# Attention and maxout FFN on one core: the first batch's K and Q by casting half-sequence loads and 32x32 turns on VectorE, with the work order written anew

## The chip, the cores and the metric

The kernel runs on one core of a Trainium2 chip. The metric is the device time of one launch in microseconds (us), the median of several runs; less is better. Engines are named as in the profile: PE (TensorE matmul), PEld (its weight load), DVE (VectorE), ACT (ScalarE), POOL (GpSimd) and SP (SyncE, which here only issues DMAs).

## The reference

Attention over 4 batches, 8 heads, 768 positions and head width 64. "Retrieval" heads (heads 0, 2 and 6 of this draw; the flags are an input) are causal; the others are causal and keep only the first 4 positions (the sink) and a window of the last 64. The result, laid out as 3072 tokens of 512, goes through an FFN that takes the maximum of three products:

```python
scores = scale * np.matmul(q, k.transpose(0, 1, 3, 2))
scores = np.where(mask[None, :, :, :], scores, -1000000000.0)
a = np.exp(scores - max); a = a / (np.sum(a, axis=-1, keepdims=True) + 1e-09)
x = np.matmul(a, v)                       # then tokens x (heads * 64)
h = np.maximum(np.maximum(x @ w1, x @ w2), x @ w3)
out = h @ w_out
```

Inputs and output are fp32; the kernel computes its products in fp16 with fp32 sums.

## The kernel before

**Tiles.** A batch is cut in two halves of 384 positions. A task t is one half of one batch with four heads: t = 4 * batch + 2 * half + quad, 16 tasks in all. Each has two pairs of heads, i = 0 and 1. The scores of a task are taken in units u (two in a first half, four in a second), each a few 128-row blocks of keys against up to 384 queries.

**Steps of a task.** K and Q must stand with the head width on the partitions. `scores` (matmul at L441) writes PSUM tiles "st" (two buffers, or single banks "st1"); ACT takes the exp into "pt" (L452). The mask is added before the exp for t = 0 and 1, as a matmul with the identity (L425); for the others the exp is multiplied by 0 or 1 afterwards (`masks`, L479), on POOL or, for eight listed cases, on DVE. `prep_v` casts v into "va" and multiplies it by the head's flag into "vf" (L392, L394). `av` multiplies pt with va or vf (L495), DVE takes the reciprocal (L503) and the product "x" (L505). x is transposed to "xT" by a DMA (L514), or by PE with a copy for t = 0, 1 and 3 (`turn_x`, L527, L531). Once a half's four pairs are in xT, a generator `ffn` is queued: 18 units of four matmuls (L338), of which those with w1 are copied by ACT into "acc" (L346) and the other two maxed by DVE (L349), then three outputs of six matmuls (L364), copied out by ACT (L370) and stored. `fill(n)` runs the next n steps of the queued generators. PSUM outside "st" comes from four banks that turn round.

**K and Q.** Batches 1 to 3: `load` casts four heads to fp16 in the DMA (POOL's queue), 768 positions at once, and `turn` transposes 32x32 blocks on DVE (L190), four instructions for a task's K and Q; the head width then stands as 2 x 32 rows, and scores run on four row tiles of 32 rows with two matmuls each (r = 0, 1). Batch 0: `load_pairs` loads fp32 pairs of heads on SP's and ACT's queues (second half on POOL's), `cast_pair` casts them to fp16 on ACT, POOL or DVE (L139), `turn_pair` transposes by PE (L157) and copies from PSUM (L162); scores run on two row tiles of 64 rows.

**Order.** The kernel is scheduled by hand: each engine runs its instructions in the order in which the Python emits them and waits at each for its inputs. The first four score units and the work around them are written out as calls; from t = 2 on a table `PROGRAM` holds for each score unit how many FFN units are due and what else to emit, and a running sum hands out `fill`. SP's loads of later v wait behind a "gate", a tiny DMA that reads a pt tile. POOL also issues the casting DMAs, in order with its other work.

Of the kernel before, what the change touches and what calls it, by code (L numbers as in the profile page):

```python
# [38 lines left out]
APART = [(0, 0, 1, (384,), 128, 0), (1, 1, 1, (384,), 128, 0)] + MASKED[1][1:]  # L39

# [11 lines left out]
def kernel(  # L52
# [31 lines left out]
    G = 4  # L84
# [4 lines left out]
    BY_DMA = (2, 4, 5, 6, 7, 8, 9, 10, 11, 12, 13, 14, 15)  # L89

    consts = ctx.enter_context(tc.tile_pool(name="consts", bufs=1))
    stage = ctx.enter_context(tc.tile_pool(name="stage", bufs=3))
    half16 = ctx.enter_context(tc.tile_pool(name="half16", bufs=3))
# [27 lines left out]
    def load_pairs(half, hp, n, engines, alone=False):  # L121
        for nm, src, eng in zip(("ks", "qs"), (k, q), engines):
            st = stage.tile([P, 4, HB, D], FP32, tag=nm, name=nm)
            m = 2 if alone else 2 * n
            for h in range(0, 2 * n, m):
                eng.dma_start(
                    out=st[:, h : h + m],
                    in_=src[
                        0, 2 * hp + h : 2 * hp + h + m, half * HALF : (half + 1) * HALF
                    ].rearrange("h (p j) d -> p h j d", p=P),  # L130
                )
            for i in range(n):
                staged.setdefault((half, hp + i), []).append(st[:, 2 * i : 2 * i + 2])

    def cast_pair(half, hp, engines):
        cast[half, hp] = []
        for nm, src, op in zip(("kn", "qn"), staged.pop((half, hp)), engines):
            x = half16.tile([P, HB, 2, D], FP16, tag=nm, name=nm)
            op(out=x, in_=src.rearrange("p h j d -> p j h d"))  # L139
            cast[half, hp].append(x)  # L140

    def of_pair(hp):
        return KQs[0, hp // 2].rearrange("p i t two -> p i (t two)")[
            :, hp % 2
        ].rearrange("p (i t) -> p i t", i=2)

    def turn_pair(half, hp, *engines):
        if (0, hp // 2) not in KQs:
            KQs[0, hp // 2] = qkt.tile([P, 2, S, 2], FP16, tag="KQ", name="KQ")
        xs = cast.pop((half, hp))  # L150
        n = 2 // len(engines)
        for part, op in enumerate(engines):
            tr = bank([P, 1024], FP16, "tr")
            for i in range(n):
                for j in range(HB):
                    c = i * HALF + j * P
                    nc.tensor.transpose(  # L157
                        tr[:, c : c + P],
                        xs[part + i][:, j].rearrange("p h d -> p (h d)"),
                        ident,  # L160
                    )
            op(  # L162
                out=of_pair(hp)[
                    :, part : part + n, half * HALF : (half + 1) * HALF
                ].rearrange("p i (t j) -> p i t j", j=HB),
                in_=tr[:, 0 : n * HALF].rearrange("p (i j t) -> p i t j", i=n, j=HB),
            )


# [12 lines left out]
    def turn(b, qd, i, part):  # L182
        if (b, qd) not in KQs:
# [5 lines left out]
        src = st[:, i, j0:j1].rearrange("c j d -> c (j d)").bitcast(FP32)  # L189
        nc.vector.transpose(  # L190
            out=dst.rearrange("c (p j) -> c j p", j=n)[:, j0:j1],
# [11 lines left out]
    def load_v(b, half, engines=None):  # L203
        engines = engines or (nc.sync,) * HB
        vs = stage.tile([P, H, HB, D], FP32, tag="vs", name="vs")
        for j in range(HB):
            r0 = half * HALF + j * P
            engines[j].dma_start(
                out=vs[:, :, j], in_=v[b, :, r0 : r0 + P].rearrange("h p d -> p h d")
            )  # L210
        staged_v[b, half] = vs
# [515 lines left out]
```

The softmax here doesn't subtract the row's maximum and nothing guards it: scores larger than these inputs give would overflow.

## Time and profile before

| | us |
|---|---|
| median of 3 runs | 200.86 (200.83 to 201.8) |
| span of the profiled execution | 199.3 |
| PE / DVE / ACT / POOL busy | 189.7 / 122.5 / 131.7 / 123.3 |
| first exp of scores (ACT L452) | starts 8.59 |
| first FFN's w1 products (PE L338) | start 17.8, run on from 18.66 |
| second FFN's start (PE L338) | 50.08 |
| last PE instruction ends | 195.7 |

The profile has the span of its execution, first to last instruction, but no other time for it; the median lies 1.56 us above. A row of the page such as "PE 7897..." gives the busy share in tenths over 40 slices of 5 us. A row of a timeline is: start, duration, engine, line, operation, output <- input, shapes, count, and in brackets the idle time ahead of it with what ended it. Rows with a count above one merge instructions that run on.

### The profile page before, as it was taken

The numbers are of one execution on the slowest core, as the hardware profiler recorded it, in microseconds if no ns is written. First come the engines' busy times: TensorE is split into PE (matmuls) and PEld (weight loads), VectorE is DVE, ScalarE is ACT, GpSimd is POOL, SyncE is SP. The second block draws the span as 40 slices with busy tenths as digits, with TensorE's granted clock in tenths as the row PEclk, the third lists the DMA queues.
The fourth block names the chain that finished last, engine by engine and source line by source line (L and its number), as shares of the span: only waits on it lengthen the run. The fifth ranks groups of instructions, "written<-read, shape, count | busy, mean of one in ns | idle before, by whom it ended". The sixth has DMA issues, their size and how long they took to land.

```text
span 199.3 us, 5133 instructions
## 1 busy us (share of the span) xinstructions
PE 189.7 (95%) x2059; PEld 109.5 (55%) x2059; DVE 122.5 (61%) x241; ACT 131.7 (66%) x206; POOL 123.3 (62%) x154
## 2 busy tenths in 40 slices
PE   7897999996999999999999999999999999999992
PEld 2455555545566465574555565565555565755652
DVE  2698587999687829861555649961555234543540
ACT  4585798786966776676786775848758769323221
POOL 3599159789887906787969635799847447400000
PEclk9999999999999999999999999999999999999999
DMA  6999999994949991904359995513410250023004
GB/s 182 270 213 245 278 238 212 213 202 112 256 81 154 194 274 43 178 0 146 95 101 132 170 254 141 85 26 98 116 23 20 105 76 20 3 64 135 3 0 158
DMA packets 43245, 26.48 MB, mean 133 GB/s; under 512 B 33558, under 2 KB 38230, under 8 KB 43222
## 3 DMA queue, kind: packets, MB, share of 16 engines
q1 hardware_dynamic: 37206, 15.01, 34.9%
q0 software_dynamic: 4784, 10.23, 26.7%
q10 hardware_dynamic: 1232, 0.92, 1.5%
q8 instruction: 16, 0.26, 0.6%
q14 instruction: 7, 0.06, 0.1%
HBM read 25.17 MB, written 6.29 MB: 158 GB/s over the span
## 4 chain that ended last, share of the span: by engine, by line
PE 78%; DVE 8%; ACT 4%; DMA 3%; issue 3%; POOL 2%; SPq 1%; ACTq 0%; POOLq 0%; DVEq 0%
PE yy L338 43%; PE yy L364 12%; PE st L441 10%; PE oacc L495 8%; DVE KQ L190 4%; PE yst L338 3%; ACT pt L452 3%; DMA ks<-in_k_dram 2%; DVE x L505 2%; DMA out_dram<-ot 1%; PE tr L157 1%; PE yst L364 1%; POOL kn L139 1%; DVE hT L349 1%; POOL qn L139 0%
## 5 line engine op out<-in xcount | busy, mean ns | idle before, releaser
L479 POOL TENSOR_TENSOR pt<-pt,mk 128x512 f16<-128x512 f16 (+1 forms) x76 | 80.6, 1084 | 34.8 <-ACT pt L452 34.7
L452 ACT ACTIVATE pt<-st 128x1024 f16<-128x1024 f32 (+3 forms) x99 | 83.1, 894 | 19.4 <-PE st L441 18.6
L349 DVE TENSOR_TENSOR acc<-yy,acc 128x384 f16<-128x384 f32 x45 | 25.1, 558 | 28.9 <-PE yy L338 19.3
L338 PE MATMUL yy<-xT,w1t 128*128 128x384 f16 x180 | 36.1, 327 | 0.1
L338 PE MATMUL yy<-xT,w0t 128*128 128x384 f16 x180 | 35.6, 326 | 0.4 <-DVE xT L531 0.4
L338 PE MATMUL yy<-xT,w2t 128*128 128x384 f16 x180 | 35.7, 327 | 0.0
L346 ACT CAST acc<-yy 128x384 f16<-128x384 f32 x45 | 21.0, 485 | 17.0 <-PE yy L338 10.5
L364 PE MATMUL yy<-woutt,hT 128*128 128x512 f16 (+1 forms) x138 | 32.0, 375 | 0.0
L441 PE MATMUL st<-KQ 32*128 32x384 f16 (+4 forms) x560 | 28.7, 279 | 1.0 <-DVE KQ L190 0.8
L349 DVE TENSOR_TENSOR hT<-yy,acc 128x384 f16<-128x384 f32 x45 | 25.1, 560 | 6.6 <-PE yy L338 4.0
L495 PEld LDWEIGHTS <-pt 128*128 128x128 f16 x672 | 24.0, 97 | 5.3 <-issue 2.1
L190 DVE STREAM_TRANSPOSE KQ<-kq 128x384 f32<-128x384 f32 x24 | 25.7, 1130 | 0.0
L338 PEld LDWEIGHTS <-w0t 128*128 128x128 f16 x192 | 18.2, 98 | 12.9 <-issue 1.0
L495 PE MATMUL oacc<-va,pt 128*128 128x65 f16 x352 | 24.8, 193 | 0.3 <-ACT va L392 0.3
L338 PEld LDWEIGHTS <-w2t 128*128 128x128 f16 x192 | 17.6, 98 | 13.3 <-issue 2.1
L338 PEld LDWEIGHTS <-w1t 128*128 128x128 f16 x192 | 17.2, 98 | 12.8 <-issue 1.3
L370 ACT COPY ot<-yy 128x512 f32<-128x512 f32 x22 | 12.9, 588 | 15.9 <-PE yy L364 9.6
L364 PEld LDWEIGHTS <-hT 128*128 128x128 f16 x150 | 14.0, 98 | 14.6 <-issue 0.3
L441 PEld LDWEIGHTS <-KQ 32*128 32x128 f16 (+1 forms) x560 | 12.2, 93 | 17.8 <-issue 11.5
L495 PE MATMUL oacc<-vf,pt 128*128 128x65 f16 x320 | 21.2, 193 | 0.8 <-POOL vf L394 0.8
L505 DVE TENSOR_TENSOR x<-oacc,rc 128x384 f16<-128x384 f32 x32 | 17.8, 557 | 1.1
L503 DVE RECIPROCAL rc<-oacc 128x6 f32<-128x6 f32 x32 | 6.1, 192 | 20.0 <-PE oacc L495 19.8
(70 smaller groups left out, 129.9 us busy)
## 6 DMA issues: line engine op xcount, KB each, us to landing
out_dram<-ot SPq DMA_DIRECT2D x23, 256.0 KB, 3.1
vs<-in_v_dram SPq DMA_DIRECT2D x21, 256.0 KB, 6.3
kq<-in_k_dram POOLq DMA_DIRECT2D x6, 384.0 KB, 5.6
kq<-in_q_dram POOLq DMA_DIRECT2D x6, 384.0 KB, 8.0
qs<-in_q_dram ACTq DMA_DIRECT2D x4, 192.0 KB, 4.0
ks<-in_k_dram SPq DMA_DIRECT2D x4, 192.0 KB, 3.6
w0t<-in_moe_w_dram POOLq DMA_DIRECT2D x1, 768.0 KB, 7.4
ks<-in_k_dram POOLq DMA_DIRECT2D x2, 384.0 KB, 7.2
```

What stands on the lines that cost most here:

```text
L190: nc.vector.transpose(out=dst.rearrange("c (p j) -> c j p", j=n)[:, j0:j1], in_=src.rearrange("c (j i) -> c j i", i=R),)
L338: nc.tensor.matmul(yy[:, 0:HALF], w_t[wi][:, ks, ni * P : (ni + 1) * P], xT[b, half][ks].rearrange("p a t -> p (a t)"), start=(ks == 0), s ...
L346: nc.scalar.copy(out=acc[ni], in_=yy[:, 0:HALF])
L349: nc.vector.tensor_tensor(out=dst, in0=yy[:, 0:HALF], in1=acc[ni], op=ALU.max)
L364: nc.tensor.matmul(yo[:, 0:n], hT[ns][:, tb * P : (tb + 1) * P], woutt[:, ns, c : c + n], start=(ns == 0), stop=(ns == NNB - 1),)
L370: op(out=ot[:, c : c + n], in_=yo[:, 0:n])
L441: nc.tensor.matmul(sts[g // m][:, g % m, c0 : c0 + n * P], KQ[rows, 0, ki * P : (ki + 1) * P], KQ[rows, 1, t0 : t0 + n * P], start=(c0 == ...
L452: nc.scalar.activation(out=pts[t, i][:, u, h0 : h0 + m, 0:w], in_=st[:, :, 0:w], func=AF.Exp, scale=sc,)
L479: engine.tensor_tensor(out=x, in0=x, in1=m, op=ALU.mult)
L495: nc.tensor.matmul(o[:, qi, hl, 0 : D + 1], pt[:, u, hl, c : c + P], vv[:, 2 * hp + hl, ki, 0 : D + 1], start=(idx == 0), stop=(idx == len ...
L503: nc.vector.reciprocal(out=rc, in_=o[:, :, :, D])
L505: nc.vector.tensor_tensor(out=x, in0=o[:, :, :, 0:D], in1=rc.unsqueeze(3).to_broadcast([P, HB, 2, D]), op=ALU.mult,)
```

## The change

- Batch 0 loads K and Q like the other batches, cast to fp16 by the DMA on POOL's queue, four heads together, but a half sequence at a time (`load_half`). Its source is h p (j d), since the half sequence cuts the heads apart. `load_pairs`, `cast_pair`, `turn_pair` and the pool "half16" go.
- `turn` turns batch 0 on DVE, one instruction for K or Q of a half. All scores run on four row tiles of 32 rows, also pair by pair.
- What was fixed in the code becomes an argument: the engine of a mask product ("k t i u d"), of an FFN copy-out ("f 1 d" or "f 1 a"), the way of xT ("av ... D" by DMA).
- The whole order is one list of items, `PROGRAM`, ahead of it a short list `FIRST`. The loads of w3 (w_t[2]) and w1 (w_t[0]) come in this order; the two others follow later. The flags' broadcast uses an own row of ones. `EARLY` is 0 and has no effect.

In the list, "s t u [i] [b]" is a score unit (of pair i alone; b: single banks), "f 1 e" one FFN step, "turn b q i half" a turn (i: 0 for K, 1 for Q), "v t i ef" a `prep_v` with the engines of its cast and product, "lh half q" a half load, "load b q" a full one, "em" and "m" the mask tables before and after the exp, "w n" a weight.

```diff
+FIRST = "lh 0 0, ir, lh 0 1, v 0 0"
+PROGRAM = (
+    "read, turn 0 0 0 0, flags, far, em 0, w 2, w 0, idle 8, turn 0 0 1 0, em 1, s 0 0 0",
+    "turn 0 1 1 0, s 0 0 1, s 0 1 0 b, v 0 0 pd, turn 0 1 0 0, em 2, s 0 1 1, v 1 0 pp, lh 1 0",
+    "v 1 1 pp, em 3, v 0 1 ad, idle 2, s 1 0 0, av 0 0, s 1 0 1, s 1 1, m 3, av 0 1, x 0 0 a",
+    "av 1 0, w 1, x 0 1 a, av 1 1, x 1 0 d, turn 0 0 0 1, turn 0 0 1 1, x 1 1 a, m 2, f 1 d",
+    "f 1 a, m 1, f 1 d, s 2 0, f 1 a, lh 1 1, f 1 a, load_vp 0 1, m 0, f 1 d, s 2 1, w 3",
+    "load 1 0, f 1 a, load 1 1, f 1 a, f 1 a, k 2 0 1 p, f 1 a, turn 0 1 1 1, turn 0 1 0 1",
+    "s 2 2, f 1 d, k 2 1 1 p, f 1 a, f 1 d, s 2 3 0, k 2 0 2 p, s 2 3 1, k 2 0 3 p, f 1 d",
+    "k 2 1 2 p, f 1 a, s 3 0, f 1 a, f 1 a, s 3 1 1, v 2 0 pd, f 1 d, gate, av 2 0 D, k 3 1 0 p",
+    "v 2 1 ap, turn 1 0 0 0, s 3 1 0, k 2 1 3 p, load_v 1 0, s 3 2 0, k 3 1 1 d, k 3 0 0 d",
...
+    "f 1 a, v 15 0 ad, f 1 d, f 1 a, k 15 1 3 d, f 1 d, k 15 0 3 p, av 15 0 D, av 15 1 D, f 1 d",
+    "f 1 a, f 1 a, f 1 a, f 1 a, f 1 a, x 15 1 a, f 1 d, f 1 a, f 1 a",
+)
...
+    def load_half(half, qd, which="kq"):
+        if (0, qd) not in staged:
+            staged[0, qd] = stage.tile([P, 2, S // R, D], FP16, tag="kq", name="kq")
+        n = HALF // R
+        for i, src in enumerate((k, q)):
+            if "kq"[i] in which:
+                nc.gpsimd.dma_start(
+                    out=staged[0, qd][:, i, half * n : half * n + n].rearrange(
+                        "p j d -> p (j d)"
+                    ),
+                    in_=src[
+                        0, G * qd : G * qd + G, half * HALF : (half + 1) * HALF
+                    ].rearrange("h (p j) d -> h p (j d)", p=R),
+                )
...
     def turn(b, qd, i, part):
...
+        if b == 0:
+            dst = dst[:, part * HALF : (part + 1) * HALF]
+            dst = dst.rearrange("c (p j) -> c j p", p=R)
+        else:
+            dst = dst.rearrange("c (p j) -> c j p", p=R)[:, j0:j1]
...
-        nc.tensor.matmul(flags, base[0:1, 0:P], RT1, start=True, stop=True)
+        nc.tensor.matmul(flags, ones, RT1, start=True, stop=True)
...
-                nc.scalar.copy(out=acc[ni], in_=yy[:, 0:HALF])
+                copy_out[0](out=acc[ni], in_=yy[:, 0:HALF])
...
-            for r in range(1 if b == 0 else 2):
-                for g in range(2 * i, 2 * i + 2) if b == 0 else range(G):
+            for r in range(2):
+                for g in [g for i in pairs for g in (2 * i, 2 * i + 1)]:
```

## The prediction

> **What bounds the kernel now.** I read the page from its head: busy shares, then the slices, then the stretches of time, then the timeline where the slices show holes.
>
> ```profile
> span 199.3 us, 5133 instructions
> PE 189.7 (95%) x2059; PEld 109.5 (55%) x2059; DVE 122.5 (61%) x241; ACT 131.7 (66%) x206; POOL 123.3 (62%) x154
> ...
> PE   7897999996999999999999999999999999999992
> ...
> DVE  2698587999687829861555649961555234543540
> ...
> DMA  6999999994949991904359995513410250023004
> ```
>
> TensorE (PE) is busy 95%, with holes in the first ten slices only, where the DMA row stands at 9 too. Busy time by stretch (PE, PEld, DVE, ACT, POOL; then clock, DMA share, GB/s):
>
> ```profile
> 18.00:37.00 19.00, 18.41 (x163) 10.13 (x162) 14.74 (x27) 15.55 (x25) 12.67 (x16) 1.00 1.13 235
> 37.00:50.00 13.00, 10.79 (x179) 6.34 (x175) 12.72 (x23) 9.54 (x14) 11.02 (x14) 1.00 0.79 169
> 50.00:90.00 40.00, 40.00 (x490) 23.86 (x479) 29.56 (x54) 29.13 (x44) 28.59 (x35) 1.00 0.78 147
> 90.00:170.00 80.00, 79.90 (x905) 45.55 (x904) 41.09 (x80) 59.30 (x90) 56.74 (x65) 1.00 0.50 100
> ```
>
> From 50 us on PE has no hole: nothing can be won there, only lost. From 37 to 50 us VectorE (DVE) is busy 12.72 of 13 us and PE only 10.79, so DVE is the bound. The timeline shows with what:
>
> ```profile
> 39.23 2.08 DVE L190 STREAM_TRANSPOSE KQ<-kq 128x384 f32<-128x384 f32 x2
> 41.84 2.08 DVE L190 STREAM_TRANSPOSE KQ<-kq 128x384 f32<-128x384 f32 x2
> 44.10 3.01 DVE L190 STREAM_TRANSPOSE KQ<-kq 128x384 f32<-128x384 f32 x3
> 48.34 1.12 DVE L190 STREAM_TRANSPOSE KQ<-kq 128x384 f32<-128x384 f32 x1
> ...
> 50.08 2.12 PE L338 MATMUL yy<-xT,w0t 128*128 128x384 f16 x12
> ...
> 54.28 1.16 POOL L479 TENSOR_TENSOR pt<-pt,mk 128x512 f16<-128x512 f16 x1 [0.94 <-ACT pt L452]
> 54.73 0.99 DVE L479 TENSOR_TENSOR pt<-pt,mk 128x512 f16<-128x512 f16 x1 [0.21 <-ACT pt L452]
> ```
>
> Eight turns of batch 1 take about 1.0 us each back to back. The second FFN starts at 50.08, with scores up to t=5, u=0 done. **I measure the change at that mark.** What PE has left there takes to the end, 149.2 us, in either kernel. The last two lines are a DVE mask product of 0.99 us that starts while POOL runs one; at 27.58, POOL idle, it takes 0.42.
>
> The transfers by form:
>
> ```profile
> 8.00:10.00 2.00, 1.87 (x20) 0.87 (x17) 1.95 (x7) 1.41 (x3) 1.36 (x4) 1.00 1.39 218
> 15.00:16.50 1.50, 1.20 (x33) 1.01 (x29) 1.35 (x5) 1.22 (x4) 1.50 (x3) 1.00 1.04 357
> 24.00:27.00 3.00, 2.92 (x27) 1.40 (x26) 2.46 (x6) 2.41 (x3) 1.20 (x3) 1.00 1.15 241
> 36.00:40.00 4.00, 4.00 (x75) 2.61 (x72) 3.97 (x7) 3.01 (x4) 2.40 (x4) 1.00 1.08 213
> ```
>
> The last number is GB/s written: v in 256-byte pieces 218, fp32 K and Q uncast 357, casting loads (weights, K and Q of batch 1) 213 to 241. A cast halves the bytes at some 60% of the rate.
>
> [...] The new loads read h p (j d), slowest dimension 4; all loads before have 128. No trace of before shows such a load.
> [...]
>
> **The change part by part.**
>
> *PE.* 48 K/Q transposes go: 24 before 12 us, beside waits, and 24 from 20.9 to 31 us (0.80 + 0.44 + 0.34 = 1.6 us). Batch 0's scores take the same time: a unit of four heads is 8 matmuls of 64 rows in about 0.6 us before (24.14), 16 of 32 rows in 0.56 after (as at 55.62).
>
> *DVE.* Removed: 7 copies KQ of 0.95, one of 0.56, two casts of 0.54, two xT copies: 9.0 us. Added: 8 turns (8.0 to 9.0), 15 acc copies and 7 ot copies that "f 1 d" puts on DVE (0.5 and 0.6: 11.7), masks from 10 to 33 (23 x 0.42 if free, about 1.0 if blocked: 10 to 23), 5 instead of 2 va casts, 14 instead of 2 vf products (about 8). DVE goes from 122 to about 155 us. ACT loses about 19 us, POOL 32; neither bounds PE in the long run.
>
> *DMA in the opening.* K and Q of batch 0: 3.15 MB at 357 GB/s = 8.8 us before; 1.57 MB at 213 = 7.4 after. The gain is 1.4 us, and w2 now goes ahead of w0 (0.79 MB at 213 = 3.7 us).
>
> **The walk to the mark.** (1) POOL first issues four casting loads (0.54 to 0.59 each, 2.3 us), and its constants (base, kept, ident) come 2.3 us later, so DVE is free at 5.3 instead of 2.9. The first K lands at about 4.5 (issue at 0.8, plus the shortest landing of a kq load, 4.6, less 0.9 for half the bytes). DVE then needs the flags 0.16, turn 1.0, RT/least/far 0.57, two masks 0.65, turn 1.0: 8.7. With 0.6 of PE the first exp is at 9.3 (8.59 before).
>
> (2) v 0 0 on SP shares the engines with four casts, then w2: alone it would be in at 10.7; I take 13.0. "v 0 1 ad" puts a va copy on ACT ahead of the exps of t=1, and these queue behind it: 13.6, then four exps (1.03, 1.03, 0.63, 0.63) with 0.9 of waits for PSUM to 17.8, av, 1/x, transposes and copy to 20.3. The first FFN can complete its sums at 20.3 (18.66 before). w0 lands at about 18, hidden.
>
> (3) From 19.7 (K and Q of the second half) DVE does two turns 2.1, three mask pairs 2.1 and three acc copies 1.5, to 25.4; PE waits for Q's turn and then for PSUM banks, and reaches unit 7 at about 25.5. w1 (23.3) is hidden. Twelve max (0.5), two turns, a vf product and waits for PE bring DVE to the reciprocal of "av 2 0" at 36.4 (38.54 before). POOL's mask products, queued behind DMA issues that wait on earlier landings, start at about 26, early enough.
>
> (4) From there DVE bounds as before: 8 turns 8.3, four 1/x pairs 3.0, three masks (1.3 to 3.0), xT 0.4: 13 to 14.7, so 49.4 to 51.1, and 0.7 for transposes and copy. **The mark comes at about 50.8: +0.7.** The 1.6 us of PE transposes saved vanish, because PE is not what is late.
>
> (5) After the mark DVE carries 36.6 us of work to the 17th unit of the third FFN, over 38 us of PE (97%; 29.56 of 40 before). Worst are that FFN's first nine units: DVE 12, PE 9, and four PSUM banks hold only some 2.6 us. With masks that meet POOL (nine, up to 0.6 each) I take +1.0, bounds 0 and +3. The tail is unchanged: after the last "av" six FFN groups (three units 1.95, three outputs 3.9 us) cover the last xT transfer, as the 5.2 us at 174.91 do now.
>
> Costed at nothing: the flags' own "ones" row (a memset of some 0.1 us in the wait for POOL's constants), the 8 + 2 idle matmuls instead of 10 (PE waits for loads there), and w1's place behind the half loads, which the masks on DVE hide by 2.2 us; were that cover gone, PE would wait at unit 7 for what is missing. v 1 0 is issued behind its gate at about 34 (36.56 before) and shares with casts as before; if it lands after 47, "v 4 1 ap" on ACT holds the copy of "x 3 1", and the mark slips with it.
>
> Sum: 199.3 + 0.7 + 1.0 = 201.0. The median of the runs is 1.56 above the profiled span; with that, 202.6.
>
> **Rivals.**
> - *The loads don't spread (slower still).* [...] a load is 32 packets on each of four engines at 0.139 us (a 1536-byte packet's mean in the records) = 4.4 us instead of 0.9. The first K lands near 7.9, everything follows by 2.4, and the second half's K and Q land at 24 instead of 19: the mark moves by a further 4. 206.5. For: the shape of the source. [...]
> - *DVE never idles (faster).* Its work from 19.7 to the "av 2 0" reciprocal is 14.6 us. If PE's results are always there first, it arrives at 34.4, the masks fall into POOL's pauses (1.3), and the mark comes at 47.8: −2.3. With no loss after, 198.6. It decides this way when the reciprocal starts before about 35.9. For: ACT and POOL are relieved, and the transposes are gone from DVE's wait. Against: acc copies placed behind turns that wait for landings.
> - *Tie.* The mark at 50.1 and nothing lost after: 200.9.
>
> **How the numbers follow.** Slower by the DVE sum (200.9 to 205) 0.44, most of it above 201.9; the loads don't spread 0.22; tie 0.14; faster 0.20. Half a per cent, 1.0 us, is about what a measurement of this kernel can tell from no change. Faster 0.20, same 0.18, slower 0.62. The likeliest case gives 202.6; its own range is 200.9 to 205. The range for 8 in 10 reaches into both outer cases, 199.0 to 207.5.
>
> **What would show it.** Right: the mark between 50 and 52, DVE over 90% busy from 37 to the mark and over 85% in the 40 us after, PE holes after the mark. The loads: 128 packets on four engines would show as a landing over 6 us for kq in the first 10 us. Wrong: the first exp before 8.5, the reciprocal of "av 2 0" before 35.9, or PE without a hole from 47 us on.

## The result and the profile after

The changed kernel takes 217.77 us (median of 4, 216.43 to 219.07) against 200.91 for the kernel before: ratio 1.082, 95% interval 1.0759 to 1.0881. It is slower by 16.9 us, well outside the forecast range of 199.0 to 207.5. Ratios here leave disturbed runs out, so that for one kernel below (e12) the ratio is lower than its median suggests.

The page of the changed kernel, its head and slices:

```profile
span 215.3 us, 5156 instructions
PE 195.6 (91%) x2091; PEld 110.7 (51%) x2091; DVE 147.4 (68%) x298; ACT 115.5 (54%) x167; POOL 95.0 (44%) x122
...
PE   0659889999799999999389999999999999999993
...
DVE  0293395879979879979437975988496766872640
...
PEclk9985599999999999999859999999999999999999
DMA  5999999997923997184991104701416340114004
```

PE now has two holes that before lacks: the first three slices (0, 6 and 5 where before has 7, 8 and 9) and slice 20, at 102 to 108 us. PEclk, the granted clock, falls to half twice; by its records from 14.2 to 27.9 us, and from 106.4 to 113.2 around the end of the second hole. By stretch (PE, PEld, DVE, ACT, POOL, then clock, DMA share, GB/s):

```profile
12.00:28.00 16.00, 14.23 (x123) 7.46 (x123) 8.37 (x21) 7.35 (x12) 10.80 (x17) 0.57 1.13 155
28.00:45.00 17.00, 16.38 (x166) 8.76 (x163) 12.99 (x29) 11.38 (x16) 9.15 (x11) 1.00 1.19 195
45.00:60.00 15.00, 13.72 (x223) 8.38 (x222) 13.33 (x23) 11.85 (x18) 12.11 (x15) 1.00 0.93 210
60.00:98.00 38.00, 38.00 (x443) 21.99 (x442) 33.25 (x64) 25.36 (x37) 20.04 (x25) 1.00 0.64 122
98.00:114.00 16.00, 11.85 (x108) 5.55 (x106) 8.61 (x15) 5.09 (x10) 8.41 (x12) 0.79 0.86 161
```

Where I feared VectorE, from 60 to 98 us, it is busy 33.25 of 38 us and PE has no hole at all. The loss lies ahead of 60 and at 98 to 114. The two ends of the first loss are in the timeline, the issue of the first load by POOL and what DVE waits for:

```profile
1.32 0.86 POOL L177 DMA_DIRECT2D kq<-in_k_dram  x1 [0.81 <-POOLq L627]
...
10.66 0.84 DVE L210 STREAM_TRANSPOSE KQ<-kq 128x384 f32<-128x384 f32 x1 [3.92 <-DMA kq<-in_k_dram]
...
12.89 0.85 DVE L210 STREAM_TRANSPOSE KQ<-kq 128x384 f32<-128x384 f32 x1 [0.34 <-DMA kq<-in_q_dram]
```

The turn of the first K begins 9.3 us after the load's issue. The first FFN products and the mark of the prediction, the second FFN slice, stand in PE's timeline:

```profile
29.39 2.35 PE L376 MATMUL yy<-xT,w0t 128*128 128x384 f16 x12
...
59.59 0.82 PE L376 MATMUL yy<-xT,w0t 128*128 128x384 f16 x4
```

The second loss stands in the timelines of SP, POOL and PE:

```profile
97.17 4.31 SPq L555 DMA_TRANSPOSE xT<-x  x2
...
99.11 0.59 POOL L189 DMA_DIRECT2D kq<-in_k_dram  x1
99.70 0.54 POOL L189 DMA_DIRECT2D kq<-in_q_dram  x1
...
108.32 0.48 PE L376 MATMUL yy<-xT,w0t 128*128 128x384 f16 x1 [4.15 <-DMA xT<-x]
```

The second of the two DMA transposes is issued at about 100 us, when POOL has just issued the cast loads "load 3 0"; it lands 8.6 us later (median of all transposes 2.3), and PE waits 4.15 us for it.

I measure every kernel at four points (us; "rest" runs from the second FFN slice, the prediction's mark, to the end of the span; a star: PE began the FFN, then stopped for the second half of K):

| kernel | first exp | first FFN products | second FFN slice | rest | span | median |
|---|---|---|---|---|---|---|
| before | 8.6 | 17.8 | 50.1 | 149.2 | 199.3 | 200.9 |
| after | 14.5 | 29.4 | 59.6 | 155.7 | 215.3 | 217.8 |
| e1 idle work first | 14.6 | 29.8 | 60.3 | 154.0 | 214.3 | 215.0 |
| e2 load 3 0 late | 12.7 | 22.9* | 59.7 | 150.9 | 210.6 | 211.7 |
| e3 full loads | 12.8 | 28.8 | 59.1 | 154.9 | 214.0 | 216.9 |
| e4 all three | 12.3 | 28.6 | 58.8 | 149.1 | 207.9 | 209.3 |
| e5 e4, hole filled | 12.6 | 30.8 | 61.0 | 149.1 | 210.1 | 209.4 |
| e6 half loads, hole filled | 14.4 | 24.8* | 59.8 | 149.1 | 208.9 | 209.6 |
| e7 e6, 2nd half by heads | 13.8 | 26.0 | 58.8 | 153.6 | 212.4 | 214.1 |
| e8 e7, 1st quad fp32 | 16.9 | 27.2 | 58.9 | 154.6 | 213.5 | 215.2 |
| e9 both quads fp32 | 10.8 | 29.0 | 59.2 | 149.0 | 208.2 | 209.7 |
| e10 e6, 2nd half early | 13.8 | 25.9 | 57.5 | 149.0 | 206.5 | 209.0 |
| e11 e9 by order of need | 13.0 | 28.3 | 58.5 | 149.6 | 208.1 | 209.9 |
| e12 e10, w0 ahead | 13.8 | 32.3 | 62.8 | 148.9 | 211.7 | 209.8 |
| e13 before, no idle work | 8.5 | 17.6 | 49.5 | 149.2 | 198.7 | 201.5 |
| e14 mixed | 10.8 | 33.1 | 63.3 | 149.4 | 212.7 | 214.0 |
| e15 e14, little idle work | 14.2 | 33.3 | 63.5 | 149.2 | 212.7 | 214.6 |
| e16 e14, V ahead | 11.7 | 22.9* | 59.7 | 152.2 | 211.9 | 213.1 |
| e17 before, w0 ahead | 7.6 | 22.0 | 53.6 | 149.2 | 202.8 | 205.3 |

Two columns read like constants. Where no DMA transpose holds PE for more than 0.6 us, the rest is 148.9 to 149.6 in both orders. And in the changed order the second slice follows the first products by 30.2 to 30.5 in ten of the thirteen rows without a star. In e7, e8 and e10 it takes 31.6 to 32.9; in e7 and e10 the clock is half for 3.4 us at the FFN's start, and for e8 the reason was not looked for. So the loss of 16.0 us in the span is the first exp +5.9, from there to the first products +5.7, from there to the slice −2.1, and the rest +6.5.

### The profile page after: what moved, and what is told of

Read it like the earlier page. It is cut to its first block, busy times and chain, and to the rows that moved or that the text cites. A ratio compares the mean times of both kernels' runs of the same rounds, so it can differ in the third digit from the quotient of the medians.

```text
span 215.3 us, 5156 instructions
## 1 busy us (share of the span) xinstructions
PE 195.6 (91%) x2091; PEld 110.7 (51%) x2091; DVE 147.4 (68%) x298; ACT 115.5 (54%) x167; POOL 95.0 (44%) x122
## 3 DMA queue, kind: packets, MB, share of 16 engines
q0 software_dynamic: 8560, 10.24, 30.2%
q1 hardware_dynamic: 36118, 14.23, 28.3%
## 4 chain that ended last, share of the span: by engine, by line
PE 80%; DMA 10%; POOL 3%; ACT 3%; DVE 2%; issue 1%; POOLq 0%; ACTq 0%
PE yy L376 43%; PE st L487 13%; PE yy L412 10%; PE oacc L536 9%; DMA kq<-in_q_dram 5%; DMA xT<-x 4%; PE yst L376 3%; ACT pt L498 2%; PE st L475 2%; POOL pt L520 1%; DMA out_dram<-ot 1%; DVE KQ L210 1%; DVE x L546 1%; POOL vf L444 1%; PE yst L412 1%
## 5 line engine op out<-in xcount | busy, mean ns | idle before, releaser
L520 POOL TENSOR_TENSOR pt<-pt,mk 128x512 f16<-128x512 f16 (+1 forms) x53 | 57.8, 1109 | 46.7 <-ACT pt L498 35.2
L376 PE MATMUL yy<-xT,w0t 128*128 128x384 f16 x180 | 36.7, 332 | 4.2 <-DMA xT<-x 4.2
L396 DVE TENSOR_TENSOR acc<-yy,acc 128x384 f16<-128x384 f32 x45 | 24.9, 559 | 18.4 <-PE yy L376 15.1
L376 PE MATMUL yy<-xT,w2t 128*128 128x384 f16 x180 | 36.4, 331 | 0.0
L210 DVE STREAM_TRANSPOSE KQ<-kq 128x384 f32<-128x384 f32 x32 | 32.7, 1056 | 4.3 <-DMA kq<-in_k_dram 3.9
L487 PE MATMUL st<-KQ 32*128 32x384 f16 (+2 forms) x640 | 32.9, 289 | 1.5 <-DVE KQ L210 1.5
L412 PE MATMUL yy<-woutt,hT 128*128 128x512 f16 (+1 forms) x138 | 31.6, 375 | 0.0
L536 PEld LDWEIGHTS <-pt 128*128 128x128 f16 x672 | 25.2, 99 | 4.4 <-issue 1.4
L536 PE MATMUL oacc<-va,pt 128*128 128x65 f16 x352 | 25.8, 197 | 0.0
L487 PEld LDWEIGHTS <-KQ 32*128 32x128 f16 x640 | 14.4, 94 | 21.6 <-issue 15.5
L393 ACT CAST acc<-yy 128x384 f16<-128x384 f32 x30 | 14.3, 485 | 20.4 <-PE yy L376 15.9
L376 PEld LDWEIGHTS <-w2t 128*128 128x128 f16 x192 | 17.4, 98 | 12.2 <-issue 1.3
L412 PEld LDWEIGHTS <-hT 128*128 128x128 f16 x150 | 13.7, 98 | 16.2 <-issue 1.5
L536 PE MATMUL oacc<-vf,pt 128*128 128x65 f16 x320 | 21.6, 194 | 0.3 <-POOL vf L444 0.3
L546 DVE TENSOR_TENSOR x<-oacc,rc 128x384 f16<-128x384 f32 x32 | 17.8, 558 | 1.2
L520 DVE TENSOR_TENSOR pt<-pt,mk 128x512 f16<-128x512 f16 (+1 forms) x33 | 16.9, 529 | 2.2 <-ACT pt L498 2.2
L444 POOL TENSOR_TENSOR vf<-va,far 128x384 f16<-128x384 f16 x9 | 7.7, 856 | 24.1 <-DVE va L442 12.6
## 6 DMA issues: line engine op xcount, KB each, us to landing
kq<-in_k_dram POOLq DMA_DIRECT2D x4, 192.0 KB, 11.9
w0t<-in_moe_w_dram POOLq DMA_DIRECT2D x1, 768.0 KB, 10.4
```

The source lines that it names most:

```text
L210: nc.vector.transpose(out=dst, in_=src.rearrange("c (j i) -> c j i", i=R),)
L376: nc.tensor.matmul(yy[:, 0:HALF], w_t[wi][:, ks, ni * P : (ni + 1) * P], xT[b, half][ks].rearrange("p a t -> p (a t)"), start=(ks == 0), s ...
L393: copy_out[0](out=acc[ni], in_=yy[:, 0:HALF])
L396: nc.vector.tensor_tensor(out=dst, in0=yy[:, 0:HALF], in1=acc[ni], op=ALU.max)
L412: nc.tensor.matmul(yo[:, 0:n], hT[ns][:, tb * P : (tb + 1) * P], woutt[:, ns, c : c + n], start=(ns == 0), stop=(ns == NNB - 1),)
L444: vf_engine.tensor_tensor(out=vf[j][:, hs, k0:k1, 0:D], in0=vs[:, hs, 0:1] if half == 0 else va[j][:, hs, k0:k1, 0:D], in1=far[:, hs, k0:k ...
```

## The experiments

**The rest of the run, and the first guesses at the start (e1 to e4).** e1 gives PE work from the start; e2 moves one load; e3 replaces the half loads; e4 has all three.

```diff
e1
-    "read, turn 0 0 0 0, flags, far, em 0, w 2, w 0, idle 8, turn 0 0 1 0, em 1, s 0 0 0",
+    "idle 12, read, turn 0 0 0 0, flags, far, em 0, w 2, w 0, idle 12, turn 0 0 1 0, em 1, s 0 0 0",
e2
-    "load 3 0, f 1 d, s 8 1, turn 2 1 1 1,
+    "f 1 d, s 8 1, turn 2 1 1 1,
...
-    "f 1 a, f 1 d, k 8 0 0 d, s 9 1,
+    "f 1 a, f 1 d, load 3 0, k 8 0 0 d, s 9 1,
e3 (and both halves turned at once, ahead of the scores)
-FIRST = "lh 0 0, ir, lh 0 1, v 0 0"
+FIRST = "load 0 0, ir, load 0 1, v 0 0"
```

> Only the idle matmuls are changed: 12 are put ahead of everything on TensorE and the later 8 become 12, so that TensorE has work from the start to about 12 us instead of standing idle until 6.8. In the changed kernel's profile the granted clock is half between 14.8 and 28.5 us. Theory 'the idle start costs the clock, and the clock costs time': the clock stays at 1.0 through that stretch, and the second FFN slice (59.6 us in the changed kernel) starts 3 to 4 us earlier: 213 to 214 us. Rival 'the transfers set the pace of the start': the first FFN products still wait until about 29 us for the loads, the time stays within 1 us of the changed kernel's 217.8 whatever the clock does.

> Only the cast load of the last batch's first quad of heads (load 3 0) is moved, from just before 'av 7 1' with its DMA transpose to some ten items later, so that the transpose (xT of av 7 1, 8.6 us from issue to landing in the changed kernel against a median of 2.3) no longer runs beside a cast load. Theory 'the transpose is held up by the cast load': the transpose lands in 2 to 3 us, TensorE's wait of 4.15 us at 104 to 108 us goes and the half clock at 107 to 114 us behind it: 209.5 to 212 us. Rival 'TensorE has no ready work there anyway, or the late load delays its turns': the wait only moves to another place and the time stays above 216 us.

> The first batch's K and Q are loaded like the other batches' (head outermost merged with the 32 rows to 128, the whole sequence in one transfer for a quad of heads) and turned in both halves at the start; the half-sequence loads are gone. Theory 'four heads outermost put a load on four DMA engines only, and that is most of the loss': K of the first quad, twice as many bytes, lands under 6.5 us after its issue instead of 9.3, the first exponential is at 11 to 13 us instead of 14.5, the first FFN products before 27 us instead of 29.4, and the time is 211 to 215 us. Rival 'it is the bytes and the shared queue, not the spread': the first K lands at over 10 us and the time is 217 us or more.

> The three edits together: whole-sequence loads of the first batch, the idle matmuls from the start, load 3 0 moved later. Theory that the loss is the spread of the loads, the half clock and the wait at 104 us, and that they add: 203 to 207 us. Rival 'they all hide one another behind the same late weights': above 209 us, with the first FFN products no earlier than 27 us.

e1: 215.04 us. The clock was full from 6.9 to 13.7 us, then half all the same until 30.7; the start did not move (slice at 60.3). The rival's account of the start held, but not its time: it said within 1 us of 217.8, and e1 takes 2.8 less. The profiled execution shows 1.7 of that in the rest (3.4 us of half clock behind the late transpose instead of 6.8).

e2: 211.73 us, 6.0 us less than after. The wait at 104 to 108 is gone, and the rest falls from 155.7 to 150.9; of the 1.9 that remain, 1.5 are a smaller wait for xT at 82 us. In e4, e5, e6, e9 and e10 no transpose holds PE, and the rest is 149.0 to 149.1. In e7, e8 and e16 PE waits 2.8, 4.0 and 2.9 us for xT at 83 us. POOL's cast loads of batch 2 and SP's transposes meet ahead of that, but they do so in after, e4 and e6 too, without a wait there; so its cause is open. **That the cast load "load 3 0" makes the DMA transpose beside it late is shown.** By what way it does so is not shown. In after the packets of the first transpose begin 1.2 us after its issue, those of the late one 4.1 us, when 183 of the load's 256 packets have begun.

e2 also runs the start of the changed kernel a second time, since its edit acts only at 100 us. The two executions differ: in e2 the first exp comes at 12.7 (14.5 in after), the clock is full from 11.2 to 28.2 us, where after has half, and from the first exp to the first FFN products it takes 10.3 us instead of 14.9. And yet the second slice comes at 59.7 (59.6 in after). PE had to stop for the second half of K; in the chain of e2 two loads of 192 KB take 21.1 of the first 27.3 us:

```profile
1.32 7.88 DMA kq<-in_k_dram
...
14.07 13.23 DMA kq<-in_k_dram
```

So a full clock alone gained nothing at the slice while the second half landed this late. And single executions of one start differ by nearly 2 us at the first exp, which limits what a single profile below can tell. The turn of the first K begins 7.7 to 9.3 us after the issue in the seven profiles with the same four half loads in front (after, e1, e2, e6, e7, e10, e12); after's is the longest.

e3: 216.93 us, a miss in the total but not in its mechanism. Queue rows of the changed kernel and of e3, in this order:

```profile
q0 software_dynamic: 8560, 10.24, 30.2%
```

```profile
q0 software_dynamic: 4912, 10.23, 25.7%
```

The same bytes take 3648 packets less: in the changed kernel each of the eight half loads adds 384 packets of 4 bytes (3072 of the 3648), and its first data packets run about four at a time (4.0 to 4.4 at 3.9 to 4.9 us, and 16.2 at 8.0 to 8.5, with all four half loads issued). A full load has more: in before the last one of batch 2 shows 16.8 at a time from 67 to 68 us. With full loads the first K, twice the bytes, was there about 5 us after its issue (5.3 in e3, 5.1 in e4, 4.9 in e5), not 7.7 to 9.3; VectorE's timeline of e4, where POOL issues at 1.30:

```profile
6.37 2.09 DVE L206 STREAM_TRANSPOSE KQ<-kq 128x384 f32<-128x384 f32 x2 [0.21 <-DMA kq<-in_k_dram]
```

That one half load keeps to four packets at a time to its end is my estimate from these counts; its later landing is measured. But a full row holds 24 neighbouring positions, so both halves must be turned before the first score: 4.2 us of VectorE instead of 1.7. The first exp came at 12.8, and the FFN hardly earlier: its first products at 28.8 (29.4 in after), where the theory had them before 27.

e4: 209.26 us, above its 203 to 207 and in its rival's range (above 209). The edits do not add: with the rest at 149.1 everything left, 8.7 us, is ahead of the second slice.

**The half clock (e5, e6).** In e3 the page grants the full clock throughout the start:

```profile
PEclk9999999999999999999969999999999999999999
```

Yet the mask matmuls from 11 to 28 us take as long in e3 (first line) as in e4 (second), where PEclk shows 5; in e6 (third) the clock is full:

```profile
L471 PE MATMUL st<-mk,ident 128*128 128x256 f16 x14 | 4.4, 402 | 1.2 <-DVE mk L323 0.6 <-ACT pt L494 0.6
```

```profile
L471 PE MATMUL st<-mk,ident 128*128 128x256 f16 x14 | 4.3, 403 | 1.6 <-DVE mk L323 1.0 <-ACT pt L494 0.6
```

```profile
L475 PE MATMUL st<-mk,ident 128*128 128x256 f16 x16 | 3.1, 274 | 0.8 <-ACT pt L498 0.8
```

402 ns against 274 (275 in before): e3 ran at half clock, and its records merely begin at 29.4 us. The column after the count is the busy sum, then the mean of one. So the clock row is to be checked against a matmul of known size. The stretches at half clock in the records last 3.4 us (e7, e16, e17), 6.8 and 13.7 (after) or 17.1 (e4, e14). What raises the clock again is not shown: in after it stayed at half for 13.7 us, though the profile has PE busy for 100% and 98% of the first two 3.4 us of them, and in e4 it stayed for 17.1 us with one such stretch at 100%; in before the records begin at 7.2 us, at full, behind 3.4 us that were busy 91%. In after and e14 it rose again 1.5 and 1.4 us ahead of the FFN, so it can rise during attention there too.

```diff
e5 (from e4)
-em 0, w 2, w 0, idle 12, turn 0 0 1 0,
+em 0, w 2, w 0, idle 22, turn 0 0 1 0,
e6 (after with load 3 0 late, 12 idle matmuls first)
-em 0, w 2, w 0, idle 8, turn 0 0 1 0,
+em 0, w 2, w 0, idle 27, turn 0 0 1 0,
```

> As the kernel with all three edits, but 22 idle matmuls instead of 12 between the flags and the first scores, so that TensorE has no hole before the first scores at 11.5 us. There the clock fell to half at 12.6 us, after the hole of 9.1 to 11.5, and the matmuls of the first two attention tiles ran at half rate until 29.7 (a mask matmul of 256 columns every 0.21 us). Theory 'the hole lets the clock fall, and the sparse attention matmuls do not raise it again: the start is TensorE at half clock': the clock stays full from 6 us on, the first FFN products start at 21 to 23 us instead of 28.6, the second FFN slice at 51 to 54 instead of 59, and the time is 201 to 204.5 us against 209.3. Rival 'the exponentials and VectorE's turns set the pace there': the first FFN products at 27 us or later, the time above 207.5 us.

> The changed kernel [...] with load 3 0 late, 12 idle matmuls at the start and 27 instead of 8 before the first scores: the clock is kept full there too. Theory 'two limits lie side by side at the start, the half clock and the landing of the second half of K': the clock stays full, but the turn of the second half, which VectorE has ahead of the last copies to xT, still waits for a landing at 27 to 29 us, so the first full FFN stretch starts at 28 to 30 us and the time is 208 to 211 us. Rival 'the half clock alone': first FFN products at 23 to 25 us and a time of 203 to 205.

e5: 209.36 us, no gain. The clock held to 16.5 us. PE then stood twice: 2.86 us, to 18.3, for masks that DVE makes behind its turns of the whole rows, and 2.15 us, to 22.25, for V, which was issued at 1.2 and was there only at 21.6. V is a third gate, which I had not listed.

e6: 209.61 us, as its first theory says. From PE's and DVE's timelines:

```profile
24.83 2.20 PE L376 MATMUL yy<-xT,w0t 128*128 128x384 f16 x12
30.30 0.64 PE L487 MATMUL st<-KQ 32*128 32x384 f16 x16 [3.27 <-DVE KQ L210]
```

```profile
27.89 0.84 DVE L210 STREAM_TRANSPOSE KQ<-kq 128x384 f32<-128x384 f32 x1 [3.19 <-DMA kq<-in_k_dram]
```

At full clock the FFN starts 10.4 us after the first exp (14.9 in after, 16 in e3 and e4), and then PE waits for the second half of K, which POOL issued at 15.9 and which lands at 27.9, 12.0 us later. **Half clock and late second half lie side by side; taking one away leaves the other.**

**The second half of K and Q (e7, e10).** e7 splits each of its loads into four of one head; e10 issues it behind the first half.

```diff
e7
+            for g in range(G if half else 0):
+                nc.gpsimd.dma_start(
+                    out=staged[0, qd][
+                        R * g : R * g + R, i, half * n : half * n + n
+                    ].rearrange("p j d -> p (j d)"),
+                    in_=src[
+                        0, G * qd + g, half * HALF : (half + 1) * HALF
+                    ].rearrange("(p j) d -> p (j d)", p=R),
+                )
e10
+    "lh 1 0, lh 1 1, idle 12, read, turn 0 0 0 0,
...
-v 1 0 pp, lh 1 0",
+v 1 0 pp",
```

> The same, and the second half of K and Q in four transfers of one head each (32 partitions outermost) instead of one transfer of four heads: 16 issues on GpSimd instead of 4. Theory [...]: K's second half lands within 8 us of its issue (13 before), before 24 us, VectorE does not wait for it, and with the clock full the FFN runs from 23 to 25 us on: 203 to 206 us. Rival 'the landing is late because of the weights queued ahead on the same queue, or the added issues hold up GpSimd': the landing stays at 26 us or later, or GpSimd's work before it comes some 8 us later, and the time stays at 208 us or more.

> As the kernel with half-sequence loads, late load 3 0 and idle matmuls up to the first scores (12 and 27), but the loads of the second half are issued right behind those of the first, at 7 to 10 us instead of 16 to 20. In that kernel the clock was full, the FFN began at 24.8 us, and then TensorE waited 3.3 and VectorE 3.2 us for the second half of K. Theory 'the landing of the second half is the limit that remains there': no such wait, the second FFN slice at 56 to 57 us instead of 59.8 and a time of 204.5 to 207 us against 209.6. Rival 'the earlier loads only push back the first ones, V or the weights': first exponential later than 15.5 us or the FFN's start later than 27, and 208.5 us or more.

e7: 214.13 us. DVE no longer waits for K: it turns the second half at 25.8 us (27.9 in e6), 11.9 after POOL issued its first head. How much sooner the loads by heads land is not shown by that. And POOL pays, as the rival said. Its timeline:

```profile
23.02 0.49 POOL L177 DMA_DIRECT2D kq<-in_q_dram  x1 [4.28 <-DMA w0t<-in_moe_w_dram]
```

With 16 issues instead of 4, POOL's issues wait for earlier loads to land (w2, then w0), and its third cast of V behind them starts at 23.5 instead of 17.4; xT costs 2.8 more. e10: 208.97 us, the wait for K is gone and the slice at 57.5, 2.3 better than e6; the median moved only 0.6, and with these intervals (1.0384 to 1.0494, 1.0342 to 1.048) that is no measured gain. What PE waits for next is w0:

```profile
25.93 3.63 PE L376 MATMUL yy<-xT,w0t 128*128 128x384 f16 x12 [1.05 <-DMA w0t<-in_moe_w_dram]
```

**Data early by another way (e8, e9, e11, e12).** e8 loads the first quad's first half as fp32 by heads and casts it on ACT, e9 both quads (the second cast on POOL); e11 puts e9's transfers in the order of need; e12 is e10 with w0 ahead of w2.

```diff
e8 (first quad; e9, e11 also the second)
+            for i, (src, eng) in enumerate(((k, nc.sync), (q, nc.scalar))):
+                for g in range(G):
+                    eng.dma_start(
+                        out=kf[R * g : R * g + R, i],
+                        in_=src[0, g, 0:HALF].rearrange("(p j) d -> p (j d)", p=R),
+                    )
...
+        nc.scalar.copy(
+            out=staged[0, 0][:, i, 0 : HALF // R].rearrange("p j d -> p (j d)"),
+            in_=staged["f32"][:, i],
+        )
e11 (from e9)
-    "lh 1 0, lh 1 1, idle 12, c0 0 0 a, c0 0 1 a, c0 1 0 p, c0 1 1 p, read, ... em 0, w 2, w 0, idle 18,
+    "idle 12, c0 0 0 a, c0 0 1 a, c0 1 0 p, c0 1 1 p, w 0, lh 1 0, read, ... em 0, w 2, idle 14,
e12 (from e10)
-em 0, w 2, w 0, idle 27,
+em 0, w 0, w 2, idle 27,
```

> As the kernel with the second halves by heads, and the first half of the first quad loaded as float32 on the SP and ACT queues, one head per transfer, and cast by ScalarE, which is idle until the first scores; the rest of the change stays (turns on VectorE, four row tiles, the new order). 14 idle matmuls before the first scores. Theory 'what is lost is the start alone: with the first scores at 9 to 10 us and a full clock the new order is as good as the old': first exponential before 11 us, first FFN products at 19 to 21.5, second FFN slice at 50 to 53, and 199 to 203 us. Rival 'the new order itself costs, for instance VectorE with 298 instructions instead of those of before': above 204 us although the first exponential is before 11 us.

> The first halves of both quads of the first batch are loaded as float32, one head per transfer, on the SP queue (Q of the first quad on ACT's), the flags ahead of them, and cast by ScalarE (first quad) and GpSimd (second quad); the second halves are issued by GpSimd as soon as its constants are done, at about 3 us instead of 15 to 19. The turns on VectorE, the four row tiles and the new order stay; load 3 0 is late, 12 + 18 idle matmuls. Theory 'the loss at the start is only that data comes late, the new order costs nothing after that': first exponential at 10 to 12 us, first FFN products 10.4 us later (as in the kernel with half-sequence loads and a full clock), that is at 20.5 to 22.5, second FFN slice 30 to 31 later at 51 to 53.5, and with 149 us after that 201 to 204 us. Rival 'with the first exponential early, another wait ends last (V, weights, masks)': first FFN products more than 12 us after the first exponential, time above 205.

> As the kernel with both quads' first halves as float32, but issued in the order of need: Q of both quads on ACT's queue, V behind K on SP's, and on GpSimd first the casts of the second quad, then w0, then the second half of the first quad, w2 only behind that, and the second half of the second quad as late as in the changed kernel. In the run before, V landed only at 19.3 us and the second quad at 12.8 and 15.9. Theory 'the DMA engines are full from 2 to 30 us in every version, so the start is set by how many bytes stand ahead of what the FFN needs': about 3.9 MB (first halves 1.57, V 0.79, w0 1.57) are read by 16 to 18 us, first exponential at 9.5 to 11 us, first FFN products at 19.5 to 22, second FFN slice at 50 to 53 and 199 to 202.5 us. Rival 'the turns and the casts hold the start': first FFN products at 25 us or later although V, K, Q and w0 landed before 19, and 205 us or more.

> As the kernel with half-sequence loads whose second halves are issued early, but w0 is issued ahead of w2 (both 0.79 MB written, 1.57 MB read). There the FFN's first products waited 1.05 us for w0 and the clock fell to half for 3.4 us behind it. Theory 'order of need': w0 lands 3 us or more earlier, the FFN starts at 24.9 us instead of 25.9, the clock stays full, second FFN slice at 54.5 to 55.5 instead of 56.5 to 57.5, and 206 to 207.5 us against 209. Rival 'w2 is then late instead': the wait only moves to w2's first products, time within 0.7 us of 209.

e8, e9 and e11 missed their times. e8 (215.20): the flags stood behind four loads on SP and landed at 10.05; behind them PE ran its 14 idle matmuls at half clock to 15.9, while DVE had Q turned by 12.7, so the first exp came at 16.9, in part for this idle work. e9 (209.74): first exp at 10.8, as meant, then 18.2 us to the FFN: the second quad was cast at 12.8 and 15.9, V landed at 19.3, and the clock fell at 15.1. e11 (209.89): V landed at 15, but eight issues on ACT's queue pushed its table load to 6.5 to 7.8 and the first exp to 13.0; the clock fell at 11.2, and from exp to FFN it took 15.3. e12: 205.60, 207.34, 212.21 and 213.41, with mean clocks of 1.0, 0.992, 0.968 and 0.966. The two quicker ones average 206.5, inside the theory's 206 to 207.5 and clear of e10 (ratio 1.0265, 1.0208 to 1.0322, against 1.0439); the two slower ones lose more than that again. The only profile is of the slowest, with V landing at 23 us, so what the quick ones do is not seen. The best, 205.6, is 4.5 above the 201.1 of before measured beside it. In that profile e12's first exp (13.8) is 5.2 us later than before's; that this makes up the 4.5 is not shown.

**What the half clock costs alone (e13), and V (e14 to e17).**

```diff
e13 (from before)
-    idle_work(8)
...
-    idle_work(2)
e14 (from e6; first quad fp32 as in e8)
+    "lh 0 1, w 0, lh 1 0, idle 12, c0 0 0 a, c0 0 1 a, read, turn 0 0 0 0, flags, far, em 0, w 2, idle 18, turn 0 0 1 0, em 1, s 0 0 0",
e15 (from e14): without "idle 12", and "idle 8" for "idle 18"
e16 (from e14)
-    "lh 0 1, w 0, lh 1 0, idle 12,
+    "lh 0 1, idle 12,
...
+s 0 1 0 b, v 0 0 pd, w 0, lh 1 0, turn 0 1 0 0,
...
+x 1 0 d, x 1 1 a, m 2, f 1 d, f 1 a, m 1, f 1 d, turn 0 0 0 1, turn 0 0 1 1, s 2 0,
e17 (from before)
+    load_weight(0)
     cast_pair(0, 0, (act, act))
```

> The kernel before with its 10 idle matmuls left out (8 ahead of the flags, 2 behind), nothing else. Its loads, casts and order are unchanged. Theory 'attention matmuls alone do not raise the clock, and at half clock TensorE sets the start': the clock is half until the FFN has begun, the stretch from the first exponential to the first FFN products takes 13 to 15 us instead of 9.2, and the time is 204 to 206.5 us against 200.9. Rival 'the half clock is hidden behind the exponentials and the loads': within 1 us of 200.9.

> The changed kernel with the first half of the first quad as float32 (K on SP's queue, Q on ACT's, cast by ScalarE), the second quad as a cast load behind GpSimd's constants, then w0, then the second half of the first quad; V right behind K on SP's queue; load 3 0 late; 12 and 18 idle matmuls so that TensorE has no hole before the first scores. Theory 'late data and the half clock are the whole loss': first exponential at 10 to 11.5 us, clock full, first FFN products at 21 to 23, second FFN slice at 51.5 to 54, 200.5 to 203.5 us. Rival 'the new order has a cost of its own at the start, or the DMA engines are full whatever the order': first FFN products after 25 us with a full clock, above 205.5 us.

> The same without the 12 idle matmuls at the start and with 8 instead of 18 ahead of the scores, as in the changed kernel. Theory 'the half clock has its own price': the clock is half from the first scores to the FFN, 14 to 15.5 us from the first exponential to the first FFN products instead of 10.5 to 11.5, and the time is 3 to 5 us above that of the kernel with 12 and 18. Rival 'the data ends last anyway': the two differ by less than 1 us.

> As the kernel with the first quad as float32 and 12 and 18 idle matmuls (214.0 us, V there at 24 us, first exponential at 10.8), but the cast loads of w0, of the second half of the first quad and of w2 are issued by GpSimd only behind its first cast of V, and VectorE's turns of the second half stand three FFN slices later. Theory [...]: V lands at 12.5 to 15 us, w0 at 20 to 22, the first FFN products start at 21.5 to 24, the second slice at 52 to 55, 202 to 205 us. Rival 'V is late for its own sake, from its 256-byte pieces and SP's queue': V at 19 us or later, above 208 us.

> The kernel before with a single edit: the cast load of w0 is issued at about 2.6 us, ahead of GpSimd's casts of K and Q, instead of 8.1. Theory [...]: V lands at 15 to 20 us instead of 11.5 to 13, the first FFN products start 3 to 6 us later than 17.8, and the time is 203 to 207 us. Rival 'the order of issue on another queue does not matter': V and the FFN's start within 1.5 us of before, time within 1 us of 201.

e13: 201.48 against 201.17 us, ratio 1.0012 (0.9997 to 1.0027): no difference. **My theory that attention never raises the clock fell**: in before, with its transposes, masks and 64-row scores, it is up near 10 us without any idle work (in e13 four mask matmuls take 0.85 us at 7.1 and 0.49 at 11.4). In the changed order it stayed at half to 29.4 us in e3; in after and e14, where it had fallen, it rose shortly ahead of the FFN. Whether the 32-row score tiles have to do with it was not tried.

e14 (213.98) and e15 (214.57) miss by over 10 us and differ by less than 1, as e15's rival said: both stand for V. They do not price the half clock, since both were at half for most of that stretch (e14 from 14.6 to 31.7 us). POOL's timelines of e14, then of e16:

```profile
24.12 0.96 POOL L461 CAST va<-vs 128x384 f16<-128x384 f32 x2 [13.96 <-DMA vs<-in_v_dram]
```

```profile
14.01 0.58 POOL L461 CAST va<-vs 128x384 f16<-128x384 f32 x1 [4.42 <-DMA vs<-in_v_dram]
```

V's issues began at 3.4 and 3.3 us. From 12 to 22 us e14's records show 160 to 580 of its 256-byte packets (20 to 30 ns each) in 2 us beside 170 to 235 cast packets of 134 ns; in before, where V has the engines to itself at 8 us, 1706. With w0, w2 and the second half held back until V is in (e16), V lands 10 us earlier: shown by holding these loads back together. The time, 213.13, is a miss: the first products start at 22.9 as predicted, then DVE waits for the second half until 26.1 (issued at 15.3) and PE 2.9 us with it, the clock is half from 27.3 to 30.7, PE waits 2.6 us for w1, and xT costs 2.9 at 83 us.

e17: 205.26 us, +4.3 (1.0159 to 1.0274), in the range of its theory. One cast load ahead of the short packets of K, Q and V moves the first products from 17.8 to 22.0. In before PE stops once more behind them and runs on from 18.66, in e17 from 22.03; of these 3.4 us the slice (50.1 to 53.6) and the span (199.3 to 202.8) each keep 3.5, and the medians differ by 4.3. V's packets end near 16 us instead of 11.5 to 13, as the theory had it; how much of it is the late K and Q, or the half clock from 14.2 to 17.6 us, was not separated.

This is PE in e17:

```profile
22.03 3.11 PE L338 MATMUL yy<-xT,w0t 128*128 128x384 f16 x16
```

So in this run a late start arrives whole at the end in the old order too. No version tried beats the kernel before.

## Why the prediction was wrong

- **Step 1, the first K at 4.5 us, is the first that failed.** It took the shortest landing of a kq load, 4.6 us, and subtracted 0.9 for half the bytes: 3.7 from issue. The new source has four heads outermost, and its first packets run about four at a time (4.0 to 4.4 in after): it takes 9.3 us from issue in after (7.7 to 9.3 in seven profiles), where full loads, of twice the bytes, take about 5 (e3 to e5). First exp at 14.5 instead of 9.3. How much of the loss at the slice hangs on this load alone is open, as said below. That GpSimd's constants come late behind the issues was right; they left VectorE free at 6.7 (said: 5.3).
- **The rival "the loads don't spread" was right that the load is late, and lost on size.** It put the first K at 7.9, which is 7.1 from issue; measured 9.3, and the turn at 10.66. It put the second half at 24 us; measured 29. Its packet mean of 139 ns comes from a time when packets of one kind run alone; from 3.4 to 5.4 us the cast packets average 363 ns, a few of them 0.4 to 1.8 us long. It gave 206.5, though its own terms, 2.4 and a further 4 on 202.6, add up to 209.0.
- **Step 2, first FFN sums at 20.3, failed twice over**: with the load, and by the clock. From the first exp to the FFN I counted 11.0 us; at full clock it takes 10.4 (e6) and 10.3 (e2, the same start as after), measured 14.9 at half clock. No term for the clock stood in the sum: the profile of before grants 1.0 at every stretch that I read, and the idle matmuls were "costed at nothing".
- **Step 3, the reciprocal of "av 2 0" at 36.4**: 46.66, carried over from step 2; its own stretch from the first products took 17.3 instead of 16.1. From the first products on the order is quicker than before's by 2.1 us (30.2 against 32.3), which leaves of the +11.6 there +9.5 at the slice.
- **Step 4, VectorE bounds from there to the mark, held.** From 46.66 to 59.59 VectorE is busy 12.34 of 12.93 us (95%) and PE 11.65. The sum had 13.7 to 15.4 for it, 0.8 to 2.5 too long. From 37 us on, the stretch named as the sign, it is 19.50 of 22.60 (86%, not over 90%), because that takes in part of step 3. Steps 3 and 4 together come to 30.5 forecast and 30.2 measured because the two errors cancel: partly luck.
- **Step 5, +1.0 after the mark for VectorE's load, is 0.** "What PE has left there takes 149.2 us in either kernel" was right to 0.4. What came in instead was not VectorE but the 4.15 us for one transpose and the half clock behind it, 6.5 in all. The prediction had V share the engines with casts, and did not ask the same of the other small transfers that the new order moved next to "load 3 0": the DMA transpose there had no term in the sum, and it landed after 8.6 us.
- The rivals "DVE never idles" and "tie" fell with step 1.

How the +9.5 of the start splits between first K, half clock, second half and V is not settled: each hid behind another. Shown are the longer landing of the first K (7.7 to 9.3 us against about 5 in e3 to e5), the second half's wait (e6 and e10), V's wait (e14 and e16), and the pace at half clock (402 against 274 ns); the price of the half clock by itself was not isolated, since e13 kept its clock. e2 and after bound it from one side: the same start at full and at half clock reaches the slice at 59.7 and 59.6, so behind a second half that lands at 27 to 29 us the full clock alone gains nothing.

## What to carry to other kernels

Before a DMA's shape is changed, look at its slowest dimension: with four rows outermost a load of 192 KB began with about four packets at a time (4.0 to 4.4) and took two to two and a half times as long as the sum had it (7.7 to 9.3 us for 3.7), while the page's DMA share still read 9. At a crowded start several transfers end within a few microseconds of each other, so an experiment that removes one gate shows the next; put down the landing of each (K, Q, V, weights, flags) before removing any. And ask of every small transfer that stands beside a long cast load how late it may land: V and one DMA transpose lost 6 to 10 us that way here. And compare two executions of the same code before a difference between two kernels is explained: after and e2 share their start, and lie 1.8 us apart at the first exp.

## What the runs showed of the hardware

- The granted clock on the page read 1.0 where no record existed yet: e3 was at half clock until 29.4 us with PEclk at 9. The duration of a matmul of known size told it (402 ns for a mask matmul, 274 in e6 at full clock).
- A busy PE did not always get its clock back at once: it stayed at half for 13.7 us in after, whose first two stretches of 3.4 us were busy 100% and 98%, and for 17.1 us in e4. This was seen in the changed order only, and why is open.
- Each half load with four heads outermost put 384 packets of 4 bytes on the queue beside 128 of data (queue rows of after and e3), and the first data packets ran 4.0 to 4.4 at a time (after, 3.9 to 4.9 us), where a full load showed 16.8 (before, 67 to 68 us).
- In e14 V's 3072 packets of 256 bytes, 3.6 us of work at the 1706 in 2 us of before, took up to 20 us to land beside cast packets of 134 ns. In after the DMA transpose beside a cast load had its first packet 4.1 us after its issue, the one ahead of it 1.2 us.
